# Attention ahead of two expert layers on one core: unpadded queries on array quarters, bfloat16 masks from memory, values loaded one pair late, matmuls of ones ahead of the first scores

## The chip, the cores and the metric

One Trainium2 chip (trn2), one NeuronCore of it. The metric is the device time of one launch in microseconds (us). The kernel is written with a tile framework that places each instruction on its engine's queue ahead of time; on the chip each engine works its own queue strictly in the order shown below.

## The reference, cut to what matters

Attention over 2 batches, 8 heads, 576 positions, head size 64, then two expert layers on the attention's output. Only the attention is touched by the change.

```python
scores = scale * np.matmul(q, k.transpose(0, 1, 3, 2))
mask_local = (rel >= 0) & (rel < 32)
mask_strided = (rel >= 0) & (pos[None, :] % 32 == pos[:, None] % 32)
masks = [mask_local if h < H // 2 else mask_strided for h in range(H)]
scores = np.where(masks, scores, -1000000000.0)
attn = softmax(scores)          # row maximum, exp, sum, divide
out = np.matmul(attn, v)
x = _moe_ref(out)               # 8 experts on all rows, gate normalized 8 times
return _moe2_ref(x)             # top 2 of 8 experts for each row
```

## The kernel before, in words

**Attention.** Heads go in pairs: pairs 0 and 1 are local, pairs 2 and 3 strided. A local block is 64 queries of each head against 96 keys; a strided block is 54 queries of each head against 54 keys (three residue classes). A *unit* (`unit`, L211 to L242) is three or four blocks of a pair; there are 3 units per pair, 12 per batch, 24 in all. I number them 1 to 24 in program order: 1 to 6 local and 7 to 12 strided of batch 0, then 13 to 18 and 19 to 24 of batch 1.

The steps of a unit: a matmul of the identity with the mask starts the score bank `sc` (L215), one matmul per block adds the scores (L218): the stationary operand is 128 or 108 query columns in which the two heads stand block-diagonally with zeros between them. VectorE takes the negated row maximum `nmx` (L224, L225). ScalarE makes one exponential `s` per block (L228). VectorE inverts the sums `sm` (L229, L230), GpSimd multiplies (L231), TensorE transposes into `tr` (L234), VectorE copies to `at` (L209), TensorE multiplies with the values into `ot` (L240). The result is split into a high half `xh` on ScalarE (L103) and a low half `xl` on VectorE (L105). The score banks are "a" and "d", two buffers each, taken in turn in batch 0 (`where`, L180); in batch 1 bank "a" alone (L284).

**Loads.** `load_pair` (L182) puts keys, queries and values of a pair on SyncE's DMA queue (SP): `ks`, `qs` (for most pairs a slice of `acc`) and `vs`. All four pairs of batch 0 are asked for at once. The constants `cs` come by ScalarE's queue (L264) with identity and masks in float32; VectorE casts both to bfloat16 (L266, L268).

**What stands beside the attention.** The first expert's weights come in pieces `raw` (L132 of `fetch_u`, printed as in_u, two buffers); `conv_u1` and `conv_u2` split a piece into `u1h`, `u2h` on ScalarE (L103) and `u1l`, `u2l` on VectorE (L105). `pair1` (matmuls `h`) needs the attention's output of all four pairs, chunk by chunk, and `pair2` (matmuls `y`) follows. The gate's weight `wg` (L277, L286) is loaded by ScalarE's queue and split there. The gate's normalization (`sinkhorn`) ends in nine scalings of `acc` on ScalarE (L610), among the first matmuls of the second expert (L637).

**What sets the order.** The framework's scheduler places all these on the engine queues; there is no order written by hand in this part. An instruction on a queue waits for its operands, and all behind it on that engine wait with it.

Of the kernel before, what the change touches and what calls it, by code (L numbers as in the profile page):

```python
# [47 lines left out]
B11, B21, B22, T1, T2, T3, T4 = range(7)  # L48
C_ID, C_ML = 0, 128
C_MS = C_ML + 3 * LK  # L50
C_U = C_MS + GK
C_B = C_U + 128
# [8 lines left out]
@with_exitstack  # L61
def tile_kernel(ctx: ExitStack, tc: tile.TileContext, qL, kL, vL, qS, kS, vS, wg, u12, w1, w2, wgn, noise, v1, v2, cst, dummy, out):
    nc = tc.nc
# [118 lines left out]
    def load_pair(b, hp):  # L182
        local = hp < 2
        nq, nk, nb, q, k, v = (128, LK, NJ, qL, kL, vL) if local else (2 * GK, GK, NG, qS, kS, vS)
        hp %= 2
        flip[1] ^= 1
        qs = acc[:, 4:].rearrange("p t d -> p (t d)")[:, flip[1] * 1280:flip[1] * 1280 + nb * nq]
        w = k.shape[-1]
        if b == 0 and not local:
            qs = pre.tile([128, NG * 2 * GK], F32, name=f"qs{hp}")  # L190
# [20 lines left out]
    def unit(nq, nk, mask, j0, nb, qs, ks, vs, step):  # L211
        half = nq // 2
# [22 lines left out]
        at = apool.tile([128, 4 * 2 * GK], F32, tag="at", name="at", bufs=3)  # L235
        evac(at[:nk, :nb * nq], tr[:nk, :nb * nq])
        ot = ps("c", "ot")
        for i in range(nb):
            for h in range(2):
                nc.tensor.matmul(ot[h * D:(h + 1) * D, i * half:(i + 1) * half], vs[:nk, j0 + i, h * D:(h + 1) * D],  # L240
                                 at[:nk, i * nq + h * half:i * nq + (h + 1) * half], start=True, stop=True)
        return ot  # L242

    def attention(b):
        pairs = [load_pair(b, hp) for hp in range(4)] if b == 0 else None
        for hp in range(4):
            got = pairs[hp] if pairs else load_pair(b, hp)
            if hp < 2:
                for j0, nb in LOCAL:
                    first = maskb[:, :3 * LK].rearrange("p (b k) -> p b k", b=3)  # L250
                    mask = first if j0 == 0 else first[:, 1:2].to_broadcast([128, nb, LK])
                    ot = unit(128, LK, mask, j0, nb, *got, NQ)
                    o = slice(b * S + j0 * NQ, b * S + (j0 + nb) * NQ)
                    split(xh[:, hp, o], xl[:, hp, o], ot[:, :nb * NQ])
            else:
                view = [x[:, hp, b * S:(b + 1) * S].rearrange("p (i r) -> p r i", r=STRIDE) for x in (xh, xl)]
                for j0, nb in STRIDED:
                    mask = maskb[:2 * GK, None, 3 * LK:].to_broadcast([2 * GK, nb, GK])
                    ot = unit(2 * GK, GK, mask, j0, nb, *got, GK)
                    r0, r1 = j0 * GR, min((j0 + nb) * GR, STRIDE)  # L260
                    split(view[0][:, r0:r1], view[1][:, r0:r1],
                          ot[:, :(r1 - r0) * NI].rearrange("p (r i) -> p r i", i=NI))

    nc.scalar.dma_start(cs[:, :C_U], cst[:, :C_U])  # L264
# [302 lines left out]
    for q in range(NP):  # L567
        raw = fetch_u(0, q)
        a, b = conv_u1(raw[0]), conv_u2(raw[1])
# [461 lines left out]

_HOST = ["qL", "kL", "vL", "qS", "kS", "vS", "wg", "u12", "w1", "w2", "wgn", "noise", "v1", "v2", "cst", "dummy"]


def layout(x):
# [13 lines left out]
    def queries(a, n):
        t = keys(a).reshape(B, 2, 2, D, -1, n)  # L1050
        o = np.zeros((B, 2, 2, D, t.shape[4], 2, n), a.dtype)
        for h in range(2):
            o[:, :, h, :, :, h] = t[:, :, h]
        return o.reshape(B, 2, 2 * D, -1)

# [17 lines left out]
    p, c = np.arange(128)[:, None], np.arange(128)[None, :]  # L1073
    cst[:, C_ID:C_ID + 128] = p == c
    i, c2 = p % NQ, np.arange(LK)[None, :]
    band = (c2 >= i + 1) & (c2 <= i + STRIDE)
    for j in range(3):
        ok = band & (c2 >= STRIDE) if j == 0 else band
        cst[:, C_ML + j * LK:C_ML + (j + 1) * LK] = np.where(ok, 0.0, MASKED)
    i, c2 = np.arange(2 * GK)[:, None] % GK, np.arange(GK)[None, :]  # L1080
    ok = (i // NI == c2 // NI) & (c2 <= i)
    cst[:2 * GK, C_MS:C_MS + GK] = np.where(ok, 0.0, MASKED)
    cst[:, C_U:C_U + 128] = p < c
# [32 lines left out]
```

## Time and profile before

| what | value |
|---|---|
| median of 3 runs | 1129.99 us (1126.79, 1129.99, 1136.73) |
| profiled execution, device time | 1126.98 us |
| its span, first to last instruction | 1125.0 us |
| TensorE busy, of the span | 1095.7 us, 97% |
| VectorE, ScalarE, GpSimd busy | 59%, 35%, 16% |
| mean granted TensorE clock | 0.994 |

The profile is one execution. A timeline gives start, duration, engine, line, operation and tiles of an instruction, in brackets the idle time of the engine before it and what ended that. A float32 matmul of the scores stands as two records. SPq and ACTq are instructions that start a DMA. "PE" is TensorE, "DVE" VectorE, "ACT" ScalarE, "POOL" GpSimd. Records of matmuls overlap; the distance from start to start is what a matmul takes of the engine.

### The profile page before, as it was taken

To read this page: it belongs to the slowest core of one execution; us is meant where nothing else is said; L and a number is where in the kernel's file an instruction comes from. 1 tells how busy PE (TensorE), PEld (TensorE's weight loads), DVE (VectorE), ACT (ScalarE), POOL (GpSimd) and SP (SyncE) were. 2 spreads that over 40 slices of the span, in tenths; PEclk is the share of its full clock that TensorE was granted. 3 is DMA by queue.
4 is the path that set the end of the run, shared out by engine and by line. 5 is a ranking of instruction groups with operands and counts; after the bars stand their busy time and mean duration, and the time that the engine had idled before them with its cause. 6 is when DMAs were issued, how large, how long until landed. Compare 5 with 4: busy or idle time off the path is not lost.

```text
span 1125.0 us, 16986 instructions
## 1 busy us (share of the span) xinstructions
PE 1095.7 (97%) x6683; PEld 959.7 (85%) x6683; DVE 664.7 (59%) x1362; ACT 393.7 (35%) x884; POOL 185.2 (16%) x221
## 2 busy tenths in 40 slices
PE   7999999999999999999999999999998999999996
PEld 6787988999898998899988999899787788888885
DVE  5876795676666766666666666643356364544440
ACT  5631334333322333223332233221133263544441
POOL 3410132111111111211111110000041411222211
PEclk9999999999999999999999999999999999999998
DMA  9711152111111111111111111021122782555541
GB/s 304 217 52 73 38 174 86 38 63 50 38 39 38 55 59 38 38 38 51 64 38 39 38 46 68 4 109 38 57 48 76 175 318 27 195 194 194 171 100 23
DMA packets 31071, 98.71 MB, mean 88 GB/s; under 512 B 6506, under 2 KB 14954, under 8 KB 22412
## 3 DMA queue, kind: packets, MB, share of 16 engines
q1 hardware_dynamic: 16028, 80.52, 20.7%
q0 software_dynamic: 5200, 10.17, 4.5%
q10 hardware_dynamic: 9760, 6.89, 2.0%
q8 instruction: 54, 0.88, 0.3%
q14 instruction: 29, 0.24, 0.1%
HBM read 86.06 MB, written 11.60 MB: 87 GB/s over the span
## 4 chain that ended last, share of the span: by engine, by line
PE 88%; DVE 5%; DMA 3%; ACT 2%; issue 1%; SPq 0%; POOL 0%; POOLq 0%; DVEq 0%; ACTq 0%
PE y L163 42%; PE h L163 16%; PE a L637 13%; PE b L637 7%; PE d L637 3%; PE y L809 2%; DMA raw<-in_u 1%; PE xgt L722 1%; DMA qs<-in_qS 1%; DVE wl L105 1%; DMA wg_sb<-in_wg 1%; DVE u1l L105 1%; DVE acc L565 0%; PE ot L240 0%; ACT acc L610 0%
## 5 line engine op out<-in xcount | busy, mean ns | idle before, releaser
L561 DVE SCALAR_TENSOR_TENSOR acc<-y,P,acc 128x512 f32<-128x512 f32 x216 | 159.4, 748 | 147.0 <-PE y L163 147.0
L163 PE MATMUL y<-u2h,gh 128*128 128x512 f32 x504 | 198.5, 394 | 0.4 <-DVE acc L561 0.4
L163 PE MATMUL y<-u2l,gh 128*128 128x512 f32 x504 | 197.5, 392 | 0.0
L163 PE MATMUL y<-u2h,gl 128*128 128x512 f32 x504 | 189.8, 392 | 0.4 <-DVE gl L101 0.3
L153 POOL TENSOR_TENSOR ut<-raw 128x256 f32<-128x256 f32 x48 | 35.0, 751 | 509.8 <-DVE u1l L105 430.0
L163 PEld LDWEIGHTS y<-u2h,gl 128*128 128x128 f32 x504 | 94.4, 188 | 20.9 <-DVE gl L101 1.7
L163 PE MATMUL h<-xl,wh 128*128 128x384 f32 (+8 forms) x352 | 110.8, 315 | 0.0
L163 PE MATMUL h<-xh,wh 128*128 128x384 f32 (+8 forms) x352 | 109.9, 315 | 0.6 <-ACT xh L103 0.3
L163 PE MATMUL h<-xh,wl 128*128 128x384 f32 (+8 forms) x352 | 110.1, 313 | 0.0
L163 PEld LDWEIGHTS y<-u2h,gh 128*128 128x128 f32 x504 | 94.8, 188 | 15.8 <-issue 0.8
L163 PEld LDWEIGHTS y<-u2l,gh 128*128 128x128 f32 x504 | 94.8, 188 | 14.2
L100 ACT ACTIVATE hh<-h 128x256 fp32r<-128x256 f32 (+2 forms) x88 | 35.8, 415 | 99.8 <-PE h L163 96.0
L163 PEld LDWEIGHTS h<-xh,wh 128*128 128x128 f32 x352 | 66.5, 190 | 2.0 <-DVE hl L101 0.6
L163 PEld LDWEIGHTS h<-xl,wh 128*128 128x128 f32 x352 | 66.6, 189 | 1.5 <-issue 1.0
L103 ACT ACTIVATE u2h<-raw 128x1024 fp32r<-128x1024 f32 x31 | 32.9, 1061 | 98.9 <-PE y L163 98.9
L163 PEld LDWEIGHTS h<-xh,wl 128*128 128x128 f32 x352 | 66.6, 189 | 0.3 <-issue 0.2
L101 DVE SCALAR_TENSOR_TENSOR hl<-h,hh 128x256 fp32r<-128x256 f32 (+2 forms) x88 | 40.5, 464 | 38.8 <-ACT hh L100 37.0
L637 PE MATMUL a<-sh,u1h 128*128 128x288 f32 x192 | 57.4, 299 | 2.7 <-ACT s L643 2.7
L105 DVE TENSOR_TENSOR wl<-raw,wh 128x1024 fp32r<-128x1024 f32 x42 | 49.5, 1221 | 17.6 <-ACT wh L103 17.6
L637 PE MATMUL a<-sh,u1l 128*128 128x288 f32 x192 | 57.3, 298 | 0.0
L637 PE MATMUL a<-sl,u1h 128*128 128x288 f32 x192 | 57.1, 298 | 0.0
L637 PE MATMUL b<-sh,u1h 128*128 128x288 f32 x192 | 56.7, 295 | 0.0
(245 smaller groups left out, 2497.7 us busy)
## 6 DMA issues: line engine op xcount, KB each, us to landing
raw<-in_u SPq DMA_DIRECT2D x31, 1024.0 KB, 4.7
raw<-in_v SPq DMA_DIRECT2D x20, 1024.0 KB, 8.9
acc<-in_v SPq DMA_DIRECT2D x12, 1024.0 KB
raw<-in_w SPq DMA_DIRECT2D x4, 1024.0 KB
out<-zero ACTq DMA_DIRECT2D x1, 3072.0 KB
x2d<-acc ACTq DMA_DIRECT2D x9, 256.0 KB, 2.0
vs<-in_vL SPq DMA_DIRECT2D x4, 432.0 KB, 10.1
acc<-in_qL SPq DMA_DIRECT2D x3, 576.0 KB
```

What stands on the lines that cost most here:

```text
L100: seen[0] = nc.scalar.activation(hi, src, AF.Relu)
L101: nc.vector.scalar_tensor_tensor(lo, src, 0.0, hi.bitcast(F32), op0=ALU.max, op1=ALU.subtract)
L103: seen[0] = nc.scalar.activation(hi, src, AF.Copy)
L105: nc.vector.tensor_tensor(lo, src, hi.bitcast(F32), op=ALU.subtract)
L153: nc.gpsimd.tensor_tensor(t[:, o], x, y, op=ALU.subtract)
L163: nc.tensor.matmul(o, a, b, start=start, stop=stop)
L561: nc.vector.scalar_tensor_tensor(acc[:, t], p, P[:, t, scale:scale + 1], acc[:, t], op0=ALU.mult, op1=ALU.add)
L637: nc.tensor.matmul(p, l[:, b, c], m, start=first and i == 0, stop=i == 5, skip_group_check=not first)
L722: nc.tensor.transpose(p[:, o:o + k], xg[:k, c * 128:(c + 1) * 128], ident[:k, :k])
L809: nc.tensor.matmul(p[j * w:j * w + k, :d], hr[:, f, :k], raws[f // 4][:, f % 4, j * d:(j + 1) * d], start=f == 0, stop=f == 7)
```

## The change

Five edits of the attention, all else equal in the source:

1. Queries are loaded without the zeros between the heads (half the bytes). The scores of a block are now two matmuls, one per head, on rows and columns 0 to 63 and 64 to 127 of the array. Strided units now work on 128 rows in place of 108.
2. Identity and masks come as bfloat16 from memory in an own load; the two casts go.
3. In batch 0 the values of a pair are asked for after the keys and queries of the next pair, and the first weight piece (`fetch_u(0, 0)`) after pair 1.
4. `hum` puts matmuls of ones (512 columns) into the score bank ahead of a unit's scores: 10 for unit 1, 2 each for units 2 to 12.
5. The score bank is "a" alone from the strided pairs of batch 0 on, not only from batch 1 on.

```diff
-        nq, nk, nb, q, k, v = (128, LK, NJ, qL, kL, vL) if local else (2 * GK, GK, NG, qS, kS, vS)
+        nq, nk, nb, q, k, v = (NQ, LK, NJ, qL, kL, vL) if local else (GK, GK, NG, qS, kS, vS)
...
-        nc.sync.dma_start(vs[:nk, :nb], v[b, hp])
-        return qs, ks, vs
+        return (qs, ks, vs), lambda: nc.sync.dma_start(vs[:nk, :nb], v[b, hp])
+
+    def hum(o, n):
+        for _ in range(n):
+            nc.tensor.matmul(o, onesb, onesb[:, None, :].to_broadcast([128, 4, 128]), start=True, stop=True)
...
+        hum(sc, 10 if where[0] == 1 else 2 if where[0] <= 12 else 0)
         nc.tensor.matmul(sc[:nq, :nb * nk], identb[:nq, :nq], mask, start=True, stop=False)
         for i in range(nb):
             j = j0 + i
-            nc.tensor.matmul(sc[:nq, i * nk:(i + 1) * nk], qs[:, j * nq:(j + 1) * nq], ks[:, j * step:j * step + nk],
-                             start=False, stop=i == nb - 1)
+            for h in range(2):
+                r = slice(h * 64, h * 64 + 64)
+                nc.tensor.matmul(sc[h * 64:h * 64 + w, i * nk:(i + 1) * nk], qs[r, j * w:(j + 1) * w],
+                                 ks[r, j * step:j * step + nk], start=False, stop=i == nb - 1)
...
+    def load_first():
+        pairs, queue = [], []
+        for hp in range(4):
+            got, values = load_pair(0, hp)
+            pairs.append(got)
+            if queue:
+                queue.pop(0)()
+            queue.append(values)
+            if hp == 1:
+                ready.append(fetch_u(0, 0))
+        queue.pop()()
+        return pairs
...
+            if b == 0 and hp == 2:
+                where[1] = "a"
...
-    identb = spool.tile([128, 128], BF16, name="identb", bufs=1)
-    nc.vector.tensor_copy(identb, ident)
-    maskb = apool.tile([128, 3 * LK + GK], BF16, name="maskb", bufs=1)
-    nc.vector.tensor_copy(maskb, cs[:, C_ML:C_U])
+    maskb = mask_sb.bitcast(BF16)
+    identb = maskb[:, :128]
...
-    where[1] = "a"
     attention(1)
...
     for q in range(NP):
-        raw = fetch_u(0, q)
+        raw = ready.pop() if ready else fetch_u(0, q)
```

The scheduler moves much with these edits. Three places follow. A row is line, operation, target, sources and shape; "x3" means three in a row.

The first is SyncE's queue of DMAs, before, from the strided pairs of batch 0 to the second weight piece (raw is a weight piece; the rows after the first raw are batch 1's):

```order
L203 DMA ks_117<-in_kS 128x594
L204 DMA qs_116<-in_qS 128x1188
L205 DMA vs_118<-in_vS 54x1408
L203 DMA ks_123<-in_kS 128x594
L204 DMA qs_122<-in_qS 128x1188
L205 DMA vs_124<-in_vS 54x1408
L132 DMA raw<-in_u 128x2048
L203 DMA ks<-in_kL 128x608
L204 DMA acc<-in_qL 128x1152
L132 DMA raw<-in_u 128x2048
```

The same queue after the change, from the first weight piece to the second:

```order
L133 DMA raw<-in_u 128x2048
L204 DMA ks_116<-in_kS 128x594
L205 DMA qs_115<-in_qS 128x594
L206 DMA vs<-in_vL 96x1152
L204 DMA ks_122<-in_kS 128x594
L205 DMA qs_121<-in_qS 128x594
L206 DMA vs_117<-in_vS 54x1408
L206 DMA vs_123<-in_vS 54x1408
L204 DMA ks<-in_kL 128x608
L205 DMA acc<-in_qL 128x576
L205 DMA acc<-in_qS 128x594 x2
L133 DMA raw<-in_u 128x2048
```

The first piece moved ahead of the strided pairs; the second stayed behind them and behind three query loads of batch 1.

The second place is ScalarE's queue, before, around the two conversions of weight pieces:

```order
L103 ACTIVATE xh<-ot 128x192
L103 ACTIVATE u1h<-raw 128x512
L228 ACTIVATE s,sm<-sc,nmx 108x54 x4
L103 ACTIVATE u1h<-raw 128x512
L103 ACTIVATE u2h<-raw 128x1024
L103 ACTIVATE xh<-ot 128x192
L228 ACTIVATE s,sm<-sc,nmx 108x54 x3
L103 ACTIVATE xh<-ot 128x12x18
L103 ACTIVATE u1h<-raw 128x512 x2
L103 ACTIVATE u2h<-raw 128x1024
L228 ACTIVATE s,sm<-sc,nmx 128x96 x3
```

The same queue after the change, from its first exponentials on:

```order
L235 ACTIVATE s,sm<-sc,nmx 128x96 x9
L104 ACTIVATE u1h<-raw 128x512 x2
L104 ACTIVATE u2h<-raw 128x1024
L235 ACTIVATE s,sm<-sc,nmx 128x96 x6
L104 ACTIVATE xh<-ot 128x192 x3
L235 ACTIVATE s,sm<-sc,nmx 128x96 x3
L235 ACTIVATE s,sm<-sc,nmx 128x54 x4
L104 ACTIVATE u1h<-raw 128x512 x2
L104 ACTIVATE u2h<-raw 128x1024
L104 ACTIVATE xh<-ot 128x192 x2
L235 ACTIVATE s,sm<-sc,nmx 128x54 x7
L104 ACTIVATE xh<-ot 128x192
```

Before, the second conversion stands behind all 22 strided exponentials of batch 0; now it stands behind four of them, with 18 behind it.

The third place is VectorE's queue after the change, at the same conversion (u1l and u2l are its low halves, nmx the negated maximum on which unit 8's exponentials wait):

```order
L106 TENSOR_TENSOR u1l<-raw,u1h 128x512
L213 COPY at<-tr 96x384
L231 TENSOR_REDUCE nmx<-sc 128x4
L106 TENSOR_TENSOR u1l<-raw,u1h 128x512
L213 COPY at<-tr 54x432
L106 TENSOR_TENSOR u2l<-raw,u2h 128x1024
L232 TENSOR_SCALAR nmx<-nmx 128x4
```

Before, at that place, the maxima of all strided units of batch 0 were done and these rows stood there:

```order
L105 TENSOR_TENSOR u1l<-raw,u1h 128x512
L224 TENSOR_REDUCE nmx<-sc 128x3
L105 TENSOR_TENSOR u1l<-raw,u1h 128x512
L209 COPY at<-tr 54x432
L225 TENSOR_SCALAR nmx<-nmx 128x3
L105 TENSOR_TENSOR u2l<-raw,u2h 128x1024
L229 TENSOR_SCALAR sm<-sm 128x3
```

What moved in front of these rows is the maxima of units 8 to 12, which now come behind them.

Further on, the nine scalings of `acc` (L610 before, L637 now) stood on ScalarE's queue as six, two and one with other work between; now the nine stand in a row, after one `s<-b` of the second expert and ahead of the next.

## Rows read from the trace of the kernel before

**Rows 1.** Engines by stretch: us, busy (instructions), granted clock, DMA share, GB/s.
```profile
core 0: us, PE busy (x) PEld busy (x) DVE busy (x) ACT busy (x) POOL busy (x), PEclk, DMA share, GB/s
10.00:20.00 10.00, 8.88 (x91) 7.26 (x91) 6.93 (x28) 6.45 (x37) 3.96 (x6) 1.00 1.04 317
20.00:30.00 10.00, 9.62 (x118) 8.18 (x117) 8.90 (x31) 9.05 (x48) 3.80 (x5) 1.00 1.01 348
30.00:40.00 10.00, 9.39 (x105) 7.39 (x105) 8.49 (x26) 6.85 (x27) 3.17 (x4) 1.00 1.01 273
40.00:50.00 10.00, 9.18 (x97) 7.34 (x95) 7.99 (x23) 5.80 (x26) 5.49 (x10) 1.00 0.70 265
50.00:60.00 10.00, 10.00 (x88) 8.51 (x87) 9.05 (x26) 5.62 (x28) 3.55 (x5) 1.00 0.07 24
```

**Rows 2.** The chain of waits that ended last: start, us, what.
```profile
16.68 14.54 DMA raw<-in_u
...
35.06 8.09 DMA wg_sb<-in_wg
```

**Rows 3.** Timeline of ScalarE, 26 to 62 us.
```profile
26.01 0.33 ACT L228 ACTIVATE s<-sc,nmx 108x54 f32<-108x54 f32 x1
26.29 0.33 ACT L228 ACTIVATE s<-sc,nmx 108x54 f32<-108x54 f32 x1
...
28.60 0.37 ACT L103 ACTIVATE xh<-ot 128x192 fp32r<-128x192 f32 x1
...
31.25 1.15 ACT L103 ACTIVATE u1h<-raw 128x512 fp32r<-128x512 f32 x2 [0.95 <-DMA raw<-in_u]
32.30 1.04 ACT L103 ACTIVATE u2h<-raw 128x1024 fp32r<-128x1024 f32 x1
...
38.37 0.55 ACT L103 ACTIVATE xh<-ot 128x216 fp32r<-128x216 f32 x1 [1.68 <-PE ot L240]
...
43.18 0.23 ACT L103 ACTIVATE wg<-wg_sb 128x32 fp32r<-128x32 f32 x1 [2.15 <-DMA wg_sb<-in_wg]
...
45.77 0.34 ACT L228 ACTIVATE s<-sc,nmx 128x96 f32<-128x96 f32 x1 [2.05 <-DVE nmx L225]
...
51.22 0.31 ACT L228 ACTIVATE s<-sc,nmx 108x54 f32<-108x54 f32 x1 [0.74 <-DVE nmx L225]
```

**Rows 4.** Timeline of VectorE, the last low half of the second weight piece.
```profile
34.07 1.21 DVE L105 TENSOR_TENSOR u2l<-raw,u2h 128x1024 fp32r<-128x1024 f32 x1
```

**Rows 5.** DMA issues of the first 45 us: tiles, engine, count, size, us to landing.
```profile
raw<-in_u SPq DMA_DIRECT2D x4, 1024.0 KB
...
acc<-in_qL SPq DMA_DIRECT2D x3, 576.0 KB
...
qs<-in_qS SPq DMA_DIRECT2D x2, 594.0 KB
...
cs<-in_cst ACTq DMA_DIRECT2D x1, 235.0 KB
...
ks<-in_kL SPq DMA_DIRECT2D x1, 112.0 KB, 2.7
```

**Rows 6.** Timeline of TensorE, start and dense work.
```profile
7.86 2.85 PE L218 MATMUL sc<-ks,acc 128*128 128x96 f32 x12 [1.16 <-DMA acc<-in_qL]
...
12.61 2.22 PE L218 MATMUL sc<-ks,acc 128*128 128x96 f32 x18 [0.63 <-DMA acc<-in_qL]
...
46.22 0.39 PE L163 MATMUL h<-xh,u1l 128*128 128x512 f32 x1
46.90 0.25 PE L215 MATMUL sc<-maskb,identb 108*108 108x216 bf16 x1 [0.29 <-ACT s L228]
...
47.86 0.57 PE L240 MATMUL ot<-at,vs 96*64 96x64 f32 x12
48.36 0.86 PE L234 MATMUL tr<-cs,s 128*96 128x128 f32 x6
48.98 0.48 PE L163 MATMUL y<-u2h,gh 128*128 128x512 f32 x1
49.29 0.40 PE L163 MATMUL y<-u2l,gh 128*128 128x512 f32 x1
49.52 0.39 PE L163 MATMUL y<-u2h,gl 128*128 128x512 f32 x1
...
50.41 0.88 PE L218 MATMUL sc<-ks,acc 128*108 128x54 f32 x8
51.10 0.48 PE L163 MATMUL y<-u2h,gl 128*128 128x512 f32 x1
```

**Rows 7.** Timeline around the scalings at 169 us, ScalarE and TensorE.
```profile
169.18 3.79 ACT L610 ACTIVATE acc<-acc,P 128x512 f32<-128x512 f32 x6 [1.81 <-DVE P L331]
...
175.78 0.61 PE L637 MATMUL a<-sh,u1h 128*128 128x288 f32 x1 [2.73 <-ACT s L643]
176.19 0.44 PE L637 MATMUL a<-sl,u1h 128*128 128x288 f32 x1
176.43 0.44 PE L637 MATMUL a<-sh,u1l 128*128 128x288 f32 x1
...
180.23 0.30 PE L637 MATMUL a<-sl,u1h 128*128 128x288 f32 x1
180.36 0.30 PE L637 MATMUL a<-sh,u1l 128*128 128x288 f32 x1
```

More of the change, by code (lines that the diff above doesn't have):

```diff
@@ L48 @@
 B11, B21, B22, T1, T2, T3, T4 = range(7)
-C_ID, C_ML = 0, 128
-C_MS = C_ML + 3 * LK
-C_U = C_MS + GK
+M_ML = 128
+M_MS = M_ML + 3 * LK
+NMASK = M_MS + GK
+C_ID, C_U = 0, 128
 C_B = C_U + 128
@@ L61, in tile_kernel @@
 @with_exitstack
-def tile_kernel(ctx: ExitStack, tc: tile.TileContext, qL, kL, vL, qS, kS, vS, wg, u12, w1, w2, wgn, noise, v1, v2, cst, dummy, out):
+def tile_kernel(ctx: ExitStack, tc: tile.TileContext, qL, kL, vL, qS, kS, vS, wg, u12, w1, w2, wgn, noise, v1, v2, cst, masks, dummy, out):
     nc = tc.nc
@@ L239, in unit @@
             for h in range(2):
-                nc.tensor.matmul(ot[h * D:(h + 1) * D, i * half:(i + 1) * half], vs[:nk, j0 + i, h * D:(h + 1) * D],
-                                 at[:nk, i * nq + h * half:i * nq + (h + 1) * half], start=True, stop=True)
-        return ot
+                nc.tensor.matmul(ot[h * D:(h + 1) * D, i * w:(i + 1) * w], vs[:nk, j0 + i, h * D:(h + 1) * D],
+                                 at[:nk, (2 * i + h) * w:(2 * i + h + 1) * w], start=True, stop=True)
+        return ot
+    def load_first():
[10 more added lines that the diff above has]
+        return pairs
+    ready = []
     def attention(b):
-        pairs = [load_pair(b, hp) for hp in range(4)] if b == 0 else None
+        pairs = load_first() if b == 0 else None
         for hp in range(4):
-            got = pairs[hp] if pairs else load_pair(b, hp)
+            if pairs:
+                got = pairs[hp]
+            else:
+                got, values = load_pair(b, hp)
+                values()
+            if b == 0 and hp == 2:
+                where[1] = "a"
             if hp < 2:
                 for j0, nb in LOCAL:
-                    first = maskb[:, :3 * LK].rearrange("p (b k) -> p b k", b=3)
+                    first = maskb[:, M_ML:M_MS].rearrange("p (b k) -> p b k", b=3)
                     mask = first if j0 == 0 else first[:, 1:2].to_broadcast([128, nb, LK])
-                    ot = unit(128, LK, mask, j0, nb, *got, NQ)
+                    ot = unit(NQ, LK, mask, j0, nb, *got, NQ)
                     o = slice(b * S + j0 * NQ, b * S + (j0 + nb) * NQ)
@@ L257, in attention @@
                 for j0, nb in STRIDED:
-                    mask = maskb[:2 * GK, None, 3 * LK:].to_broadcast([2 * GK, nb, GK])
-                    ot = unit(2 * GK, GK, mask, j0, nb, *got, GK)
+                    mask = maskb[:, None, M_MS:].to_broadcast([128, nb, GK])
+                    ot = unit(GK, GK, mask, j0, nb, *got, GK)
                     r0, r1 = j0 * GR, min((j0 + nb) * GR, STRIDE)
@@ L262, in attention @@
                           ot[:, :(r1 - r0) * NI].rearrange("p (r i) -> p r i", i=NI))
+    mask_sb = apool.tile([128, NMASK // 2], F32, name="mask_sb", bufs=1)
+    nc.scalar.dma_start(mask_sb, masks)
     nc.scalar.dma_start(cs[:, :C_U], cst[:, :C_U])
-    identb = spool.tile([128, 128], BF16, name="identb", bufs=1)
-    nc.vector.tensor_copy(identb, ident)
-    maskb = apool.tile([128, 3 * LK + GK], BF16, name="maskb", bufs=1)
-    nc.vector.tensor_copy(maskb, cs[:, C_ML:C_U])
+    maskb = mask_sb.bitcast(BF16)
+    identb = maskb[:, :128]
     attention(0)
@@ L1029, in tile_kernel @@
                 down(ws[2:], [tt], [OVER], 0)
-_HOST = ["qL", "kL", "vL", "qS", "kS", "vS", "wg", "u12", "w1", "w2", "wgn", "noise", "v1", "v2", "cst", "dummy"]
+_HOST = ["qL", "kL", "vL", "qS", "kS", "vS", "wg", "u12", "w1", "w2", "wgn", "noise", "v1", "v2", "cst", "masks", "dummy"]
 def layout(x):
@@ L1047, in keys @@
         return a.transpose(0, 1, 3, 2).reshape(B, 2, 2 * D, a.shape[2])
[L1049 to L1054, printed above, removed]
     def values(a, n, step):
@@ L1074, in layout @@
     cst[:, C_ID:C_ID + 128] = p == c
+    masks = np.zeros((128, NMASK), np.float32)
+    masks[:, :128] = p == c
     i, c2 = p % NQ, np.arange(LK)[None, :]
@@ L1078, in layout @@
         ok = band & (c2 >= STRIDE) if j == 0 else band
[L1079 to L1082, printed above, removed]
+        masks[:, M_ML + j * LK:M_ML + (j + 1) * LK] = np.where(ok, 0.0, MASKED)
+    c2 = np.arange(GK)[None, :]
+    ok = (i // NI == c2 // NI) & (c2 <= i) | (i >= GK)
+    masks[:, M_MS:] = np.where(ok, 0.0, MASKED)
+    masks = (masks.view(np.uint32) >> 16).astype(np.uint16).view(np.float32)
     cst[:, C_U:C_U + 128] = p < c
@@ L1091, in layout @@
     dummy[:, 0] = np.arange(E * ROWS) % ROWS % PAD
-    d = dict(qL=queries(q[:, :4], NQ), kL=keys(kL), vL=values(vL, LK, NQ),
-             qS=queries(qS, GK), kS=keys(kS), vS=values(vS, GK, GK), wg=rows(x["moe_w_gate"]),
+    d = dict(qL=keys(q[:, :4]), kL=keys(kL), vL=values(vL, LK, NQ),
+             qS=keys(qS), kS=keys(kS), vS=values(vS, GK, GK), wg=rows(x["moe_w_gate"]),
              u12=np.stack([x["moe_w1"].reshape(E, NC, 128, NP, 256).transpose(0, 3, 2, 1, 4).reshape(E, NP, 128, 2, 512),
@@ L1098, in layout @@
              noise=x["moe2_noise"].reshape(NT, 128, E).transpose(1, 0, 2),
-             v1=w1t(x["moe2_w1"]), v2=w2t(x["moe2_w2"]), cst=cst, dummy=dummy)
+             v1=w1t(x["moe2_w1"]), v2=w2t(x["moe2_w2"]), cst=cst, masks=masks, dummy=dummy)
     return {n: np.ascontiguousarray(a) for n, a in d.items()}
```

12 lines of the change are left out of this document (6 added, 6 removed).

## The prediction, written before the changed kernel ran

> **What bounds the kernel now.** I read the engines by stretch first [rows 1]. From 50 us on TensorE is busy without a gap (10.00 of 10.00); up to 40 us the DMA engines are full (shares 1.04, 1.01, 1.01, at 317, 348 and 273 GB/s) while TensorE idles 0.4 to 1.1 us of each ten and VectorE and ScalarE are nearly as full. So there are two regimes: a start of some 47 us in which transfers, ScalarE and VectorE set the pace, and a dense part behind it. The timeline of TensorE shows the seam: the last early `h` at 46.22, a gap of 0.29 us, and then one matmul after the other [rows 6]. All of the change lies in the attention, so it is worth what it does to the moment of the seam, plus what it adds to or takes from TensorE's own work behind it. A delay of the seam reaches the end undiminished, because the dense part has next to no idle time that could take it up.
>
> The chain of waits names what sets the seam: the second weight piece `raw`, asked for at 16.68 and landed 14.54 us later, at 31.22, then the gate's weight `wg_sb`, 8.09 us [rows 2]. The timeline of ScalarE shows the links: it waits 0.95 us for `raw`, converts it from 31.25 on, then waits 1.68 us for `ot`, 2.15 us for `wg_sb` and 2.05 us for `nmx` [rows 3]. These waits, 6.8 us in all, are the slack that could swallow a small delay.
>
> **The change part by part.** The largest piece is not in the diff but in the order on ScalarE. Before, the conversion of the second piece stood behind all 22 strided exponentials of batch 0; now it stands behind four, with 18 behind it. ScalarE works in order, so these 18 now wait for a transfer of which they need nothing. I count from the landing of that piece.
>
> *Landing.* SyncE's queue ahead of that piece becomes lighter and longer. Queries are halved: 576, 576, 594 and 594 KB of batch 0 [rows 5] become 288, 288, 297 and 297, so 1170 KB less. Three query loads of batch 1 (288, 297, 297) now go ahead where one of 576 did, 306 KB more. The constants, 235 KB, become 117.5 of masks and 64 of the rest, 54 less. Together 918 KB less; at the mean of 317 and 348 GB/s [rows 1] that is 2.8 us, and the piece lands at about 28.4. If the gaps between landings eat it, 0; if the issue too comes sooner because nothing ahead waits for a buffer, -4.5. I take **-2.8**.
>
> *Work now behind the conversion.* 18 exponentials at 0.28 us (26.01 to 26.29), 5.0 us; three local `xh` of 0.37, less overlap 0.35, and one strided of 0.55 [rows 3], 1.6 us. Together **+6.6**. Bounds: 0, if waits that are there anyway hide all of it, and 6.6.
>
> *VectorE beside it.* The maximum on which unit 8's exponentials wait is finished on VectorE only behind `u2l`. Before, `u2l` ended at 34.07 + 1.21 = 35.28 [rows 4], 4.0 us after the conversion began. ScalarE itself is free after 2.1 us of conversion and two `xh` of 0.35, 2.8 us. It waits the rest, 1.2, and for the short scaling of `nmx`, together **+1.3** (0 to 2.5).
>
> *Bank "a" alone from unit 7.* Two score buffers instead of four: a unit's scores can start only after the exponentials of the unit two before it. Where the kernel already ran so, in batch 1, ScalarE waited 0.74 and 2.05 us for `nmx` [rows 3], in the mean 1.4. Six units, of which unit 8's wait is counted above; I take two more, **+2.8**, between 0 and five turns, 7.0.
>
> *The gate's weight.* Its DMA is issued by ScalarE, and ScalarE's first use of it now stands directly behind the issue. A small load, 112 KB, took 2.7 us to land [rows 5] on quiet queues; before, ScalarE waited 2.15 for `wg_sb`. So **+0.6**. If it takes 8.09 as before [rows 2], +5.9.
>
> *The first piece* goes ahead of the strided pairs and is converted among the local units. It takes about 3 us of transfer before the strided keys and queries; the values put behind make up for part. Converted early, it leaves the path; I count nothing, with the landing above already holding its bytes.
>
> *Casts.* Two casts of VectorE go, and masks come in bfloat16. TensorE's first scores waited 1.16 and 0.63 us for queries, not for masks [rows 6], so this gives nothing by itself.
>
> *Matmuls of ones.* 10 + 11 x 2 = 32 in the 12 units of batch 0, 512 columns each. The dense `y` matmuls of 512 columns start 0.23 us apart (49.29 to 49.52) [rows 6], so the ones are 7.4 us of TensorE. Ten to sixteen stand in front of the first scores, where TensorE waits for loads. The first twelve score records took 2.85 us (0.24 each), the next eighteen 2.22 (0.12) [rows 6]: TensorE begins at half its pace, though the granted clock from 10 us on reads 1.00 [rows 1], and ones in front may raise it sooner, for at most 12 x 0.12 = 1.4 us. This too vanishes while queries are awaited. The other 22 lie where TensorE waits for ScalarE: nothing. If that cover is gone, +5.0; in the sum 0.
>
> *Scores on quarters, in the dense part.* Units 19 to 24 are there. Before, a unit of four blocks took eight records and 0.69 us (50.41 to 51.10). Now it has sixteen records of half as many stationary columns. The nearest row is `ot`, with 64 columns: twelve records in 0.50 us (47.86 to 48.36), 0.042 each [rows 6]. 16 x 0.042 = 0.67, no difference. If each record keeps its 0.086, 0.69 more per unit, +4.1 for six; if the two heads run side by side, 0.34 less, -2.1. I take **0**, as the nearest row says.
>
> A page speaks against any gain here: the Trainium skill, "TensorEngine Tiling (Array Packing)", section "Restrictions and Gotchas", says that different row tiles cannot access the same PSUM bank at once, and both heads of a block write one bank `sc`. By that rule the -2.1 falls away and the sum stays as it is; the row of `ot`, whose halves also share a bank, has 0.042 per record, but its halves differ in columns alone, so no row here shows the case itself.
>
> *Transposes* of strided units grow from 108 to 128 columns: six took 0.62 us at 128 (48.36 to 48.98) [rows 6], 0.10 each. 44 records in the dense part times 0.10 x 20/108 is 0.8 at most; I take half, **+0.4**.
>
> *Scalings of `acc`.* Before, the wait for them cost TensorE 2.73 us and then matmuls at 0.24 us instead of 0.13 from 175.78 until about 180 [rows 7], some 1.3 us. Nine in a row take 5.6 us (3.79 / 6 x 9), with the `s` behind them 5.9; before, from 169.18 to the last `s` it was 6.5. It may save 0.6 or, if they begin later against TensorE, cost 1; I take 0.
>
> **Sum.** -2.8 + 6.6 + 1.3 + 2.8 + 0.6 + 0.4 = +8.9 us. The profiled execution took 1126.98 us, so 1135.9, **1136 us**. That execution stands 3.0 us below the median of the runs shown, 1129.99, and near the lowest; the forecast is for runs like it.
>
> **The rivals.** *B, absorbed.* The 6.8 us of waits of ScalarE between 31 and 46 us are there already; the 18 exponentials fill them, above all the 1.68 for `ot`, and only the bank and the scaling of `nmx` remain, about +2: 1129 us. For it: ScalarE was busy only 6.85 of 10 us from 30 to 40 [rows 1]. Against it: `wg_sb` and `nmx` are late in the chain and move with it.
>
> *C, faster: the transfers bound the start.* Eight query loads halved are 2340 KB, with the constants 2394 KB; at 0.33 MB per us that is 7 us of full queues. If the second piece lands while ScalarE is still at unit 7, by about 23 us, so that it waits less than 2 us for it, the order costs little and the seam comes earlier; net of the bank (+2) that is -5: 1122 us. For it: DMA shares above 1.00 to 40 us [rows 1]. Against it: the piece is queued behind 7.2 MB, some 22 us at 0.33 MB per us, on top of the time of the first issue.
>
> *D, slower: the gate's weight lands under load.* If its landing takes 8.09 us as before instead of 2.7, with ScalarE waiting for all of it, 5.4 us more: 1141.4. It decides if weight pieces are still in flight on the same engines when ScalarE gets to the issue, which the share of 0.70 from 40 to 50 us [rows 1] makes possible; most of that share lies early there.
>
> A rule of the page "TensorE: Matmul & The Clock Gate", section "HAM oscillation — how this bites in real kernels", is that idle gaps return the array to the slow clock. The 2.73 us gap and the 0.24 us pitch behind it [rows 7] agree; a gap of 6 us at the conversion would by the same row add about 1.3 us, to 1137.
>
> **How the numbers follow.** The forecast has 0.47, B 0.20, C 0.20, D 0.13. The forecast's own range, from the bounds of landing, bank and conversion, is +5 to +13, 1132 to 1140. For eight in ten I reach down to C, 1121, and up past D, 1145. About 1% is what a measurement of this kernel can tell from no change; from 1126.98 that is 11.3 us. Slower by more: most of D (0.11), a quarter of the forecast (0.12) and a little for the bounds of scores and ones (0.03), 0.26. Faster by more needs C with twice its gain, 0.06. Within: 0.68.
>
> **What would show it.** In the changed kernel's profile: a wait of ScalarE of 5 us or more, put down to DMA `raw`, ahead of its third and fourth `u1h` at 22 to 28 us; a gap of TensorE of about 6 us between 25 and 31; a wait of about 2.7 us for `wg_sb`; the last early `h` at 54 to 55 us instead of 46.22; TensorE's busy time up by the ones, 7 us. It would be wrong if ScalarE hardly waits for `raw`, if the seam lies at 47 us or sooner, or if the time differs while the seam does not.

## The result, and the profile after

| | before | after |
|---|---|---|
| median | 1133.25 us, 12 runs | 1141.91 us, 12 runs |
| lowest, highest | 1126.79, 1137.64 | 1139.31, 1148.32 |
| ratio after / before | | 1.0088, 95% interval 1.0061 to 1.0115 |
| profiled execution | 1126.98 us | 1140.03 us |
| its span | 1125.0 us | 1138.2 us |
| TensorE busy | 1095.7 us | 1106.7 us |

The change made the kernel 0.9% slower. The interval lies clear of 1, though single runs of either kernel scatter by about 1%. The medians differ by 8.7 us, next to the 8.9 forecast; between the two profiled executions, which the forecast was made for, it is 13.0 us.

First again the engines by stretch [rows 1] (PE, PEld, DVE, ACT, POOL busy, then granted clock, DMA share, GB/s):

```profile
0.00:10.00 10.00, 8.20 (x71) 4.47 (x71) 1.88 (x8) 3.23 (x13) 1.90 (x15) 1.00 0.80 225
10.00:20.00 10.00, 7.45 (x95) 5.14 (x94) 7.59 (x25) 6.73 (x32) 3.50 (x6) 0.88 1.03 319
20.00:30.00 10.00, 8.24 (x77) 5.54 (x75) 3.36 (x8) 2.77 (x13) 2.33 (x3) 0.78 1.02 346
30.00:40.00 10.00, 6.58 (x75) 4.69 (x76) 6.95 (x21) 5.21 (x27) 1.00 (x2) 0.66 0.66 215
40.00:50.00 10.00, 10.00 (x126) 6.89 (x124) 6.41 (x22) 5.08 (x25) 4.36 (x10) 1.00 0.08 18
50.00:60.00 10.00, 9.71 (x121) 6.83 (x121) 8.44 (x27) 6.69 (x31) 1.45 (x3) 1.00 0.17 41
```

From 20 to 30 us VectorE and ScalarE do about a third of what they did before (3.36 and 2.77 us of ten, where it was 8.90 and 9.05), with the DMA engines as full as ever: the start stands still. And the granted clock, 1.00 in all stretches of [rows 1], falls to 0.88, 0.78 and 0.66: 13.6 of these 30 us are at 1.2 instead of 2.4 GHz (twice what is missing to 1.00, times 10 us, summed). The chain of waits has the second weight piece in the same role [rows 2]:

```profile
17.72 10.84 DMA raw<-in_u
```

It lands at 28.56. The timeline of ScalarE [rows 3] shows who stands behind it:

```profile
20.92 0.34 ACT L235 ACTIVATE s<-sc,nmx 128x54 f32<-128x54 f32 x1
...
28.58 1.15 ACT L104 ACTIVATE u1h<-raw 128x512 fp32r<-128x512 f32 x2 [7.23 <-DMA raw<-in_u]
...
33.11 0.31 ACT L235 ACTIVATE s<-sc,nmx 128x54 f32<-128x54 f32 x1 [2.00 <-DVE nmx L232]
...
38.19 0.31 ACT L235 ACTIVATE s<-sc,nmx 128x54 f32<-128x54 f32 x1 [2.24 <-DVE nmx L232]
...
41.05 0.31 ACT L235 ACTIVATE s<-sc,nmx 128x54 f32<-128x54 f32 x1 [1.60 <-DVE nmx L232]
...
45.16 0.23 ACT L104 ACTIVATE wg<-wg_sb 128x32 fp32r<-128x32 f32 x1 [2.17 <-DMA wg_sb<-in_wg]
```

And that of TensorE [rows 6], with the last early `h` at 54.76 (before: 46.22):

```profile
1.13 4.98 PE L210 MATMUL sc<-onesb 128*128 128x512 bf16 x16 [1.13 <-POOL onesb L91]
...
6.53 1.70 PE L225 MATMUL sc<-ks,acc 64*64 64x96 f32 x36
...
33.42 1.95 PE L247 MATMUL ot<-at,vs 96*64 96x64 f32 x28 [5.18 <-DVE xl L106]
35.30 1.03 PE L210 MATMUL sc<-onesb 128*128 128x512 bf16 x2
...
36.44 0.99 PE L225 MATMUL sc<-ks,qs 64*54 64x54 f32 x16
37.37 0.61 PE L210 MATMUL sc<-onesb 128*128 128x512 bf16 x1
...
38.89 0.26 PE L220 MATMUL sc<-mask_sb 128*128 128x216 bf16 x1
39.08 0.61 PE L225 MATMUL sc<-ks,qs 64*54 64x54 f32 x16
39.61 0.51 PE L164 MATMUL h<-xh,u1h 128*128 128x512 f32 x1
...
50.64 0.53 PE L241 MATMUL tr<-cs,s 128*96 128x128 f32 x3
...
54.76 0.40 PE L164 MATMUL h<-xh,u1l 128*128 128x512 f32 x1
...
56.48 0.48 PE L164 MATMUL y<-u2h,gh 128*128 128x512 f32 x1
```

What the lower clock costs stands in two of these rows: sixteen score records take 0.93 us (36.44 to 37.37) in the low stretch and 0.53 (39.08 to 39.61) behind it.

**A mark to measure by.** The 73rd `h` of the first expert is the first one behind the gate's logits: in every kernel here exactly 72 `h`, 72 `y` and all 24 units lie ahead of it. It starts at 96.35 before and at 108.04 after, so 11.7 of the 13.0 us are lost by then:

```profile
96.35 0.50 PE L163 MATMUL h<-xh,u1h 128*128 128x512 f32 x1
```

```profile
108.04 0.48 PE L164 MATMUL h<-xh,u1h 128*128 128x512 f32 x1
```

The first row is of before, the second of after. TensorE's time up to the mark can be split: I add the gaps between its records (idle), the distances taken by ones, and the rest. Before it is 8.5 idle and 87.8 work; after 9.8 idle, 9.3 ones and 88.9 work. So TensorE idles only 1.3 us more than before: ones fill the first microseconds, where it waited for loads anyway (its first record starts at 1.13 instead of 4.31), and later gaps open. The same work takes 1.1 us longer, with 13.7 us at the lower clock up to the mark.

### The profile page after: what moved, and what is told of

Read it like the earlier page. It is cut to its first block, busy times and chain, and to the rows that moved or that the text cites. A ratio compares the mean times of both kernels' runs of the same rounds, so it can differ in the third digit from the quotient of the medians.

```text
span 1138.2 us, 17358 instructions
## 1 busy us (share of the span) xinstructions
PE 1106.7 (97%) x6875; PEld 958.8 (84%) x6875; DVE 665.6 (58%) x1360; ACT 393.7 (35%) x884; POOL 183.4 (16%) x221
## 4 chain that ended last, share of the span: by engine, by line
PE 87%; DVE 5%; DMA 3%; ACT 1%; issue 1%; POOL 1%; SPq 0%; POOLq 0%; DVEq 0%; ACTq 0%
PE y L164 41%; PE h L164 16%; PE a L664 13%; PE b L664 7%; PE d L664 3%; PE y L836 2%; PE xgt L749 1%; DMA ks<-in_kS 1%; DMA raw<-in_u 1%; PE sc L225 1%; PE ot L247 1%; DMA table<-en,si 1%; PE tr L241 1%; DVE u1l L106 1%; DVE acc L592 1%
## 5 line engine op out<-in xcount | busy, mean ns | idle before, releaser
L101 ACT ACTIVATE hh<-h 128x256 fp32r<-128x256 f32 (+2 forms) x88 | 35.5, 414 | 98.5 <-PE h L164 97.3
L104 ACT ACTIVATE u1h<-raw 128x512 fp32r<-128x512 f32 (+1 forms) x62 | 30.6, 541 | 80.6 <-PE a L664 57.5
L664 PE MATMUL b<-sl,u1h 128*128 128x288 f32 x192 | 57.1, 297 | 0.0
```

The costliest lines, as they stand in the source:

```text
L101: seen[0] = nc.scalar.activation(hi, src, AF.Relu)
L104: seen[0] = nc.scalar.activation(hi, src, AF.Copy)
L664: nc.tensor.matmul(p, l[:, b, c], m, start=first and i == 0, stop=i == 5, skip_group_check=not first)
```

## The experiments

The medians of the kernel before differ from one set of runs to the next (1133.3, 1136.3, 1136.1, 1131.7 us), because its executions lie in two groups, a short one up to about 1132 us and a long one from there to 1141, which the last experiment is about; the lowest of each set agree (1126.7 to 1127.1). So I compare the experiments by their own medians and by the mark. The last column is the time that the profiled execution spent at 1.2 GHz up to the mark, by its granted clock.

| kernel | median us | ratio to before, interval | mark us | idle / ones until the mark, us | at 1.2 GHz, us |
|---|---|---|---|---|---|
| after | 1141.9 | 1.0088 (1.0061 to 1.0115) | 108.0 | 9.8 / 9.3 | 13.7 |
| conv2_late | 1140.5 | 1.0043 (1.0016 to 1.0070) | 109.8 | 9.0 / 9.6 | 13.7 |
| fetch2_early | 1138.7 | 1.0037 (1.0003 to 1.0071) | 112.7 | 11.7 / 9.3 | 20.5 |
| late_front_ones | 1131.6 | 0.9961 (0.9929 to 0.9992) | 97.9 | 6.9 / 4.2 | 6.8 |
| late_banks_ad | 1137.1 | 1.0003 (0.9971 to 1.0035) | 103.8 | 6.4 / 9.8 | 6.8 |
| ones_n1 | 1140.3 | 1.0041 (1.0005 to 1.0078) | 108.5 | 10.9 / 8.0 | 13.7 |
| front_ones | 1131.9 | 0.9973 (0.9937 to 1.0008) | 98.5 | 7.8 / 4.2 | 6.8 |
| bef_ones | 1137.7 | 1.0014 (0.9980 to 1.0048) | 101.8 | 5.8 / 9.8 | 6.8 |
| late_front_banks_ad | 1132.0 | 0.9981 (0.9942 to 1.0019) | 98.9 | 7.1 / 3.6 | 6.8 |
| pinned_short_ones | 1140.7 | 1.0076 (1.0045 to 1.0107) | 106.4 | 11.5 / 5.0 | 13.7 |
| pinned_conv2_moved | 1139.1 | 1.0060 (1.0028 to 1.0092) | 104.0 | 7.5 / 8.4 | 6.8 |
| pinned_both | 1138.7 | 1.0051 (1.0019 to 1.0083) | 105.3 | 8.9 / 4.8 | 17.1 |

My theory at the outset was the prediction's: the conversion held in front of 18 exponentials costs most of it. The rival was the ones, which I had priced at nothing.

**1. The conversion moved by a dependency (conv2_late).** `exps` collects the exponentials.

```diff
-        a, b = conv_u1(raw[0]), conv_u2(raw[1])
+        if q == 1:
+            with tc.issue_after(exps[39].ins):
+                a, b = conv_u1(raw[0]), conv_u2(raw[1])
```

> The changed kernel, with the conversion of the second weight piece put behind all 22 strided exponentials of batch 0 on ScalarE (a dependency for the order alone); all else is placed by the scheduler as before. Theory (the conversion, waiting 7.2 us for its transfer in front of 18 exponentials, delays the seam): ScalarE's wait for raw falls below 2 us, TensorE's gap of 5.2 us at 28 us goes, and the time falls by 5 to 8 us from the changed kernel's 1142, to about 1135. Rival 1 (the matmuls of ones, 9 us of TensorE, are the cost, and the gap only takes their place): less than 2 us, about 1141. Rival 2 (the landing itself bounds the first early h, wherever the conversion stands): less than 2 us, and TensorE's gap moves to 35 to 45 us.

It gave 1.4 us, inside the scatter, and the mark of the profiled execution, the slowest of its ten, came 1.8 us later. The wait of ScalarE for `raw` is gone, but TensorE's gap has only moved, to 40 us, with another engine behind it. First GpSimd, then TensorE:

```profile
41.44 1.11 POOL L306 CAST upper<-cs 128x128 bf16<-128x128 f32 x1 [2.70 <-DMA cs<-in_cst]
42.50 0.43 POOL L497 CAST en<-cs 128x6 int32<-128x6 f32 x3
42.90 0.45 POOL L238 TENSOR_TENSOR s<-s,sm 128x162 f32<-128x162 f32 x1
...
43.40 0.52 PE L241 MATMUL tr<-cs,s 128*54 128x128 f32 x3 [3.45 <-POOL s L238]
```

In the new order a cast of constants (`upper`, first used by TensorE at 828 us) stands on GpSimd in front of unit 12's multiplication and waits for its own load. It is the same pattern as the held conversion, one engine further on. By time and by the place of the gap this is what the second rival expected, but not for its reason: ScalarE reaches the conversion at 37.81 without waiting for `raw`, and another queue holds the work.

**2. The transfer moved (fetch2_early).** The second piece is asked for directly behind the first.

```diff
-                ready.append(fetch_u(0, 0))
+                ready.extend([fetch_u(0, 1), fetch_u(0, 0)])
```

> The changed kernel, with the second weight piece asked for directly behind the first, ahead of the strided pairs. Theory: the piece lands by about 17 us, ScalarE waits for it less than 3 us, strided keys land 3 us later; 4 to 7 us less than the changed kernel, about 1136. Rival (transfers bound the start in any order): the wait moves from raw to the strided keys and queries, and the time stays within 2 us of 1142.

ScalarE no longer waits for this piece, but TensorE waits 2.43 us for the strided queries, and later ScalarE for the gate's weight:

```profile
18.46 0.99 PE L225 MATMUL sc<-ks,qs 64*54 64x54 f32 x16 [2.43 <-DMA qs<-in_qS]
```

```profile
45.35 0.23 ACT L104 ACTIVATE wg<-wg_sb 128x32 fp32r<-128x32 f32 x1 [6.81 <-DMA wg_sb<-in_wg]
```

The mark is the latest of all (112.7), 4.7 us behind the changed kernel, while the median is 3.2 us lower: the profiled execution, with a span of 1143.2, is the longest of its ten, and the one with most time at 1.2 GHz. The waits moved, as the rival says; the 3.2 us lie between its 2 and the theory's 4, so the price isn't settled.

**3. Fewer ones (late_front_ones, front_ones, ones_n1).** late_front_ones is experiment 1 with ones in front of unit 1 alone; front_ones the changed kernel with the same edit; ones_n1 the changed kernel with one matmul in place of two.

```diff
-        hum(sc, 10 if where[0] == 1 else 2 if where[0] <= 12 else 0)
+        hum(sc, 10 if where[0] == 1 else 0)
```

> As conv2_late, and the matmuls of ones only in front of unit 1 (10 of 32 left; 22 gone). If the ones lie in TensorE's waits, no more than 1 us below conv2_late. If they lie on the path (ScalarE waits for nmx, nmx for scores, scores for the ones ahead of them), 3 to 5 us below it: 22 x 0.22 us.

> The changed kernel with ones only in front of unit 1. Without the other 22 the scheduler itself puts the second conversion behind 19 of the 22 strided exponentials. So both costs go at once, the ones and the hold: it should stand with late_front_ones, 0.994 to 0.998 of the kernel before. If it is above 1.002, the position behind all 22 was what mattered in late_front_ones.

> The changed kernel with one matmul of ones in place of two in units 2 to 12 (21 in all); the second conversion stays behind four strided exponentials on ScalarE. If the ones lie on the path themselves (scores wait for them, nmx for the scores, ScalarE for nmx), half of their 9 us goes: 3 to 5 us below the changed kernel, about 1.005 of the kernel before. If the held conversion is the cost and the ones fill waits, the wait of about 7 us for raw and a gap of TensorE of about 5 us stay, and the time stays within 1.5 us of the changed kernel, 1.008 to 1.010.

Without the 22 later ones both kernels are 9 to 10 us faster, level with before or a little below it. That is twice what 22 matmuls of 0.24 us last. Halving them gave 1.6 us, no more than the scatter. A cost that doesn't scale with the number of matmuls is not their duration alone. What else differs is the order: in front_ones the scheduler itself puts the second conversion behind 19 strided exponentials; with one matmul each it still puts it behind four. The clock differs too, as a rival: up to the mark the traces have 6.8 us at 1.2 GHz without the later ones and 13.7 with them. Over whole runs it explains little: the median of the mean granted clocks is 0.9905 in front_ones and 0.9895 in the changed kernel, which is worth some 1.2 of the 10 us (an estimate, the missing share times the run's length).

**4. The ones alone on the kernel before (bef_ones).** The same `hum`, 32 matmuls, in the old kernel.

> The kernel before with the 32 matmuls of ones and nothing else of the change (queries padded, both conversions behind local exponentials or strided ones as the scheduler puts them). If the ones cost time by themselves, 4 to 9 us above before, 1.004 to 1.008. If only together with the hold: within 2 us, 0.998 to 1.002.

Ones in front raise the pace, as the prediction allowed: twelve score records that took 2.85 us before [rows 6] take 1.48.

```profile
8.62 1.48 PE L223 MATMUL sc<-ks,acc 128*128 128x96 f32 x12
```

The mark is 5.4 us later than in the first trace of before, but 0.7 earlier than in the second one (experiment 7), and the interval of the times holds 1. No verdict by the median. But none of its ten runs falls in the short group of the kernel before (lowest 1133.7, where 11 of 31 runs of before beside it lie below 1132), and the median granted clock is 0.989 against 0.994: so the ones alone seem to keep the old kernel out of its short group.

**5. The score bank (late_banks_ad, late_front_banks_ad).** Both banks to the end of batch 0, on experiment 1 and on late_front_ones.

```diff
-            if b == 0 and hp == 2:
-                where[1] = "a"
...
+    where[1] = "a"
     attention(1)
```

> As conv2_late, with both score banks in turn to the end of batch 0, as in the kernel before. Theory of the prediction (bank a alone costs two turns of 1.4 us): 2 to 3 us below conv2_late. If the bank is no bound once ScalarE isn't held up: within 1 us of it.

> late_front_ones with both score banks in turn to the end of batch 0. conv2_late lost about 4 us with the two banks; if the bank limits TensorE independently of the ones, 2 to 4 us below late_front_ones, 0.992 to 0.994 of before; if the bank only bound because ones sat in it, within 1 us of late_front_ones.

With the ones the second bank gives 3.4 us, without them nothing (1132.0 against 1131.6). And with both banks the 22 ones cost 5.1 us (1137.1 against 1132.0, the mark 4.9), about 22 x 0.23, as if there nothing covered them. In all of these pairs the scheduler also planned anew, so the edit is not all that differs. The clock is a rival for the 3.4 us: its median over the runs is 0.991 in conv2_late and 0.9935 in late_banks_ad, by the same estimate worth some 2.8 us.

**6. The same order, one thing changed (pinned_short_ones, pinned_conv2_moved, pinned_both).** To separate order and duration I wrote down the order of the changed kernel on all five engines and tied each instruction to the one ahead of it, by dependencies meant to set the order alone.

```diff
+        for runs in ORDER.values():
...
+                    if last is not None:
+                        tc.add_manual_dep(i, last.name, mybir.DependencyInfo(mybir.DependencyClass.NoSync, mybir.DependencyReason.DATA), reason="order")
+                    last = i
```

In the first kernel the 22 ones have 16 columns. In the second six instructions of the list move: ScalarE's `u1h`, `u1h`, `u2h` behind the issue of the `wg` load, VectorE's `u1l`, `u1l`, `u2l` behind the sums of unit 13 (the expectation below says unit 12). The third has both. No run has the tied order and neither edit; but TensorE's records come in the same sequence in all four traces, and in the second kernel their starts stay within 0.4 us of the changed kernel's up to 19.3 us.

> The changed kernel with every engine's order held, instruction for instruction, as the scheduler gave it to the changed kernel; only the 22 matmuls of ones of units 2 to 12 have 16 columns in place of 512. If each one of them is on the path: 22 x 0.24 = 5 us less than the changed kernel, about 1137 (its profiled execution 1140.0, so 1135), and the first expert's 73rd h, which in the changed kernel's trace starts 11.7 us later than in that of before, then 6 to 7 us later. If they lie in waits that the held conversion leaves: less than 1.5 us.

> The changed kernel, every engine's order held as in the changed kernel, all 32 ones in full; only the second piece's three conversions on ScalarE stand behind the issue of the wg load (where ScalarE waits 2.17 us for wg anyway) and the three on VectorE behind unit 12's sums. If the hold costs what the prediction summed (8.5 us without the transposes): 6 to 9 us less than the changed kernel, 1133 to 1136. If the path behind it is bounded by something else (ones, the first transfers): 3 us or less, 1139 or more. ScalarE's wait of 7.2 us for raw and TensorE's gap of 5.2 us should go in either case.

> Both edits at once, ones of units 2 to 12 short and the conversion moved, all other order held. If the two costs are separate and add up: the sum of the two gains, 10 to 12 us, 1130 to 1132, so the change without its ones and its hold would stand within 3 us of the kernel before. If one only covers the other: no more than the larger of the two gains.

Short ones at the same order: the mark 1.6 us earlier, the median 1.2 lower, though the ones take 4.3 us less. The wait at the conversion is still there, 5.93 us on ScalarE, where it was 7.23, and 5.22 on TensorE, where it was 5.18:

```profile
28.12 1.15 ACT L112 ACTIVATE u1h<-raw 128x512 fp32r<-128x512 f32 x2 [5.93 <-DMA raw<-in_u]
```

```profile
32.95 1.94 PE L257 MATMUL ot<-at,vs 96*64 96x64 f32 x28 [5.22 <-DVE xl L114]
```

So in this order most of the ones did lie in waits, as the prediction said. The moved conversion gives 4.0 us at the mark and 2.9 in the median; both waits it was meant to remove are gone, and a new one has come. VectorE, ScalarE, TensorE (its first two rows are the formerly held `ot` and the last record ahead of the new wait):

```profile
39.74 1.73 DVE L114 TENSOR_TENSOR u1l<-raw,u1h 128x512 fp32r<-128x512 f32 x2
41.40 1.21 DVE L114 TENSOR_TENSOR u2l<-raw,u2h 128x1024 fp32r<-128x1024 f32 x1
...
43.79 0.82 DVE L239 TENSOR_REDUCE nmx<-sc 128x3 f32<-128x288 f32 x2
```

```profile
44.80 0.34 ACT L243 ACTIVATE s<-sc,nmx 128x96 f32<-128x96 f32 x1 [4.64 <-DVE nmx L240]
```

```profile
26.04 1.23 PE L255 MATMUL ot<-at,vs 96*64 96x64 f32 x28 [0.18 <-DVE xl L114]
...
41.45 0.53 PE L249 MATMUL tr<-cs,s 128*96 128x128 f32 x3
43.94 0.56 PE L255 MATMUL ot<-at,vs 54*64 54x54 f32 x12 [1.96 <-DVE at L221]
```

The low halves, in one block of 2.9 us, now stand in front of `at` and of the maxima of two units. My move freed ScalarE and held VectorE. Because TensorE's sequence is the same, the two traces can be laid side by side, record by record. At the formerly held `ot` the moved kernel is 7.4 us ahead (26.04 against 33.42), at the transposes 9.2 (41.45 against 50.64). Of the 9.2, 2.4 had come ahead of the hold, where the changed kernel's trace is at 1.2 GHz (17.6 to 24.4 us) and this one is not, 5.0 came at the wait itself, and 1.8 in the changed kernel's second low stretch, behind its gap (31.2 to 38.0). Then the new waits take back 2.6 and a low stretch behind them (45.0 to 51.8) another 2.6, which leaves the 4.0 (the row has the columns of the first view above, 0.50 is the granted clock):

```profile
45.00:51.80 6.80, 6.60 (x44) 4.53 (x44) 3.44 (x12) 4.18 (x20) 1.33 (x2) 0.50 0.64 221
```

So in this pair of traces the hold with the low clock behind it was worth 6.8 us where it stood (5.0 and 1.8), and 2.9 in the median at the end; the 4.0 at the mark hold the 2.4 that are not the edit's. What a better place for VectorE's part would leave was not tried. Both edits together give 3.2 us in the median and 2.7 at the mark, no more than the move alone: they don't add up.

**7. The kernel before once more (before_again).**

> The kernel before once more, for a second trace of it: its runs lie in two groups, 1127 to 1130 and 1134 to 1141 us, at the same granted clock, and the first trace is of the lower group. If this trace is of the upper group, the start of the first expert's h and y beside the first trace's shows where the 8 us lie: at the start (the attention), or in a later place that the change does not touch.

1133.5 us, a span of 1131.6, and the mark at 102.47, 6.1 us later than in the first trace: the difference lies in the start, which means in the attention. The two traces part within 14 us:

```profile
8.24 2.85 PE L218 MATMUL sc<-ks,acc 128*128 128x96 f32 x12 [1.55 <-DMA acc<-in_qL]
...
13.65 4.11 PE L218 MATMUL sc<-ks,acc 128*128 128x96 f32 x18 [1.27 <-DMA acc<-in_qL]
```

The queries land 0.4 us later than in the first trace, and 18 score records take 4.11 us instead of 2.22 [rows 6], nearly twice as long each. The second weight piece is asked for 2.0 us later and lands 5.4 later:

```profile
36.61 1.15 ACT L103 ACTIVATE u1h<-raw 128x512 fp32r<-128x512 f32 x2 [3.18 <-DMA raw<-in_u]
```

So the start of the old kernel varies by some 6 us between these two executions, and my sum had been made on the short one.

## Why the prediction came out right

The forecast was 1136 us, the range 1121 to 1145, and "within 1%, leaning slower" as the likeliest; 1141.9 and +0.9% lie in it, though above the 1132 to 1140 that the bounds of its terms gave. That the medians differ by 8.7 us where the sum says 8.9 is luck: half of the 12 runs of before are of its long group, and like with like it is 13.0. By its steps:

- *Landing:* 28.4 forecast, 28.56 measured. The count of bytes ahead in the queue held for these two executions; from the second trace of before, where the piece landed 5.4 us later (experiment 7), the same count would have given 33.8.
- *The seam:* the 24th `h` is the last early one in both traces, at 46.22 and 54.76, so 8.5 us later, where 8 to 9 were forecast. But the mark is 11.7 later. The prediction's step that the change is worth the delay of the seam and little more doesn't hold: another 3.2 us come between the seam and the mark. In part they are work put off: two units of scores and twelve `ot` records that stood ahead of the seam before now stand behind it, some 2 us by their rows.
- *The hold:* a wait of 5 us or more ahead of the second conversion (7.23), a gap of about 6 us on TensorE (5.18, but at 28 to 33 us instead of 25 to 31): both there. Its price, 6.6 + 1.3, is confirmed only in place: at held order the moved conversion put TensorE 6.8 us ahead (experiment 6), of which 2.9 were left in the median, with a new wait in its place.
- *Bank "a" alone:* two turns of 1.4 us. Unit 8's wait is 2.00, and behind it come 2.24 and 1.60 for `nmx`: 3.8 where 2.8 was summed. But the bank is not what came last there: unit 8's exponentials, which free it for unit 10, ended at 34.4, and unit 10's scores started at 36.44, behind `ot` and two ones on TensorE's own queue. Experiment 5 gives 3.4 with the ones, most of which the clock could be, and nothing without. So no run shows this term by itself.
- *The gate's weight:* a wait of 2.17 us, as before [rows 3]; the +0.6 didn't come, nor rival D. That D can happen is seen in fetch2_early, with 6.81.
- *Matmuls of ones, costed at 0:* this is the step that was wrong in its reach. At the held order they are worth 1.2 to 1.6 us, a fair miss. TensorE's busy time rose by 11.0 us, not 7: up to the mark the ones take 9.3, for the first seven run at half pace and some later ones at 1.2 GHz. But I looked for them only on TensorE. They also enter the scheduler's plan: without the 22 later ones it makes an order that is 10 us shorter (1131.9 against 1141.9). That order differs in many places, the position of the conversion among them, and which of these carry the rest of the 10 us stays open.
- *The clock:* I had it as one gap worth 1.3 us, outside the sum. Up to the mark 13.7 us are at 1.2 GHz, and TensorE is busy in 10.6 of them, so up to 5.3 us of its work are lost (an estimate, half of the busy time). Against that stands the half pace of the first 12 us before, with 6.4 us busy, up to 3.2 us by the same estimate, which the ones now fill.
- *Scores on quarters, 0:* sixteen records in 0.53 us (39.08 to 39.61) against eight in 0.69 before [rows 6], so 0.16 less per strided unit of four blocks. But the mask's matmul in front now holds TensorE 0.19 us (38.89 to 39.08), where it was 0.10 (46.90 to 47.00 [rows 6]), so less than 0.1 us is left: 0 was right. The gain comes without the heads running side by side: 0.033 per record of 54 columns is the pace of `ot`'s 0.042 for 64 [rows 6]. That agrees with the Trainium skill, "TensorEngine Tiling (Array Packing)", section "Restrictions and Gotchas", that row tiles don't share a PSUM bank at the same time.
- *Transposes, +0.4:* in the dense part the strided ones start 0.109 us apart (median), where it was 0.092. There are 22 of them behind the seam, not 44, which makes 0.4 us. The size is right because I halved a count that was twice too high.
- *Scalings of `acc`, 0:* the wait there is 2.90 against 2.73 [rows 7], now put down to VectorE's `b`:

```profile
194.19 0.40 PE L664 MATMUL a<-sh,u1h 128*128 128x288 f32 x1 [2.90 <-DVE b L685]
```

Between the first expert's last `h` (163.9 before, 175.9 after) and 200 us another 1.7 us are lost; this term was missing. 1.2 of them come back between 810 and 835 us, where the trace of before has 3.4 us at 1.2 GHz and that of after has none.

Rival B fell with the 7.23 us wait, C with the landing at 28.56 instead of 23. In short: the place and the sign were right, and the held conversion is shown as one part of the loss. The size of the sum is right by luck: the first trace of before was a short execution, the hold is only in part shown, and the order that the ones brought and the clock were sized too small.

## What to carry to other kernels

An instruction that waits for a transfer holds all that stands behind it on its engine, and moving it only pays if the place where it lands holds nobody either, on every engine that has a part of it: look at all five queues, not at the one with the longest wait. A matmul that is meant to do nothing still counts where an automatic scheduler plans by it; before pricing such an addition by its duration, compare the orders with and without it. To tell order from duration in an experiment, hold the whole order fixed and change one thing.

Of the kernels tried, late_front_ones (the change with ones in front of unit 1 alone and the second conversion behind batch 0) is the fastest, 0.9961 of before (0.9929 to 0.9992) and 10 us below the changed kernel; front_ones and late_front_banks_ad are within 0.5 us of it.

## What the runs showed of the hardware

- In the first microseconds TensorE runs matmuls at half the later pitch while the granted clock column reads 1.00: 0.24 us per score record against 0.12, until about 12 us in the first trace of before and until about 17.8 in the second. With 16 matmuls of ones ahead the first score records ran at full pace (36 in 1.70 us from 6.53 on). The 1.00 in these stretches is the lack of a record: the traces' clock records begin only at 11.9 and 17.6 us, and at 3.9 in the changed kernel, where the ones go from 0.43 us apart to 0.22. So the mean granted clock leaves this start out, and the two groups of the kernel before, which have nearly the same mean, can differ in it.
- Two executions of the same program differed by 0.4 us in a landing at 8 us and by 6.1 us at 100 us. In between, the later one has the longer half pace, the second weight piece 5.4 us later and a stretch from 40 to 50 us at a granted clock of 0.66; which of these led to which was not tested. The stretch in before_again:

```profile
40.00:50.00 10.00, 9.91 (x84) 8.24 (x82) 6.65 (x23) 4.52 (x24) 4.07 (x9) 0.66 0.65 237
```
